# Token matmuls of an attention block in one run with two heads side by side, and the first loads reordered

## The chip, the cores and the metric

The kernel runs on one core of one Trainium2 chip. The metric is the device time of one execution, in microseconds (us); the median of ten runs is given. A profiled execution of the same kernel gives the trace that is read below: for each engine its instructions, their start, their duration and what they waited for. TensorE does matmuls, VectorE (DVE), ScalarE (ACT) and GpSimd (POOL) do the element work, SyncE (SP), ACT and GpSimd issue DMAs on their own queues, and instructions of one engine run in the order in which they are written.

## The reference

Linear attention without a softmax, a norm per head, and then a bilinear feed-forward layer:

```python
kv = einsum('bhsd,bhse->bhde', k, v)        # B 8, H 8, S 576, D 64
o = einsum('bhsd,bhde->bhse', q, kv)
o = o / sqrt(mean(o * o, axis=-1) + 1e-6) * g_norm
x = o.transpose(0, 2, 1, 3).reshape(4608, 512)
out = ((x @ w_a) * (x @ w_b)) @ w_out       # 512 -> 1536 -> 512
```

All inputs and the output are fp32; the kernel computes in bf16 with fp32 sums.

## The kernel before, in words

The output is made in nine strips of 512 tokens; a batch has 576 tokens, so strip s+1 needs the first tokens of batch s+1 and the last ones of batch s. The matrix that all strips read is `xt`: x transposed, 128 rows by 4 blocks by 4608 tokens, in bf16. The FFN of a strip is 12 units (`Unit`, n = 0 to 11) of two halves of four 128x512 matmuls each (L315): half a ends in a copy by ACT (L329, `part_a`), half b in a multiply by DVE (L333, `part_b`). Then come four output groups (n = 12 to 15, `ffn_o`, 12 matmuls each, L372), whose copies alternate between DVE and ACT and whose rows SP stores (L365). The PSUM memory has eight banks, `P[:, 0]` to `P[:, 7]`. From strip 1 on, the halves of the units take banks 1, 2, 0, 4 in turn (`ab_bank`), output groups bank 3 (`O`) or the next of the turn.

Batches 0 and 1 are made up front with q transposed by TensorE. Of pair 0 (two heads) of batch 0, q, k and v come as fp32 on SP's and ACT's queues and are cast by DVE and ACT (L447 to L450); the other pairs come in bf16 on GpSimd's queue (`load_pair`, three DMAs at L116 for each), which also makes the identity matrix that the transposes need (`make_identity`, a memset and a select). While TensorE waits at the start it runs matmuls of zeros (`dummy`, L400).

Batches 2 to 7 are made inside strips 1 to 6, batch s+1 in strip s, by `slot(A, s, n)`: it is called after each unit or output group n, and as `slot(A, s, n - 0.5)` between its two halves, and what it issues stands at that place in every engine's order. At n = k0 TensorE makes kv of one batch, in strips 3 and 5 of two (`kv`, L168, pairs of 128x64 tiles, into bank 7); copies put it on the diagonal of `kvb`, a 128x128 matrix per pair of heads with zeros elsewhere (`kv_out`, L179). The attention output is made in five chunks of tokens (0 to 3 of 128, and LC = 4 of the last 64): `tx` multiplies a chunk of q with `kvb`, four 128x128 matmuls (L265), and ACT squares the result (L272); `tss` sums the squares per head on DVE (L276); `trs` takes the reciprocal root on ACT (L281) and multiplies with g on GpSimd (L288); `txt` multiplies on DVE (L297) into `x_tok` and SP transposes it into `xt` by DMA (L299). The chunks' `tx` come at n = 6.5, 8, 9.5, 11, 12.5 in strip 1; in the strips 2 to 6 at x0, x0+1.5, +2.5, +4, +5 with x0 = 3.5, 5.5, 1.5, 5.5, 1.5. `tss` follows half a step, `trs` one and `txt` two and a half steps after `tx`. The banks of the chunks are 5, 6, 7 in turn.

At n = 12, 4, 8, 5, 8 of strips 1 to 5, after that step's slot, SP also issues the transposition of the next batch's q from DRAM (`transpose_q`, L151), and at n = 3 and 14 of strip 1 and at n = 10, 14, 8 of strips 2 to 4 GpSimd issues the loads of a later batch (`load_late`: a copy that waits for a transposition, L136, and six DMAs, L139 to L146).

Of the kernel before, what the change touches and what calls it, by code (L numbers as in the profile page):

```python
# [8 lines left out]
FP32 = mybir.dt.float32  # L9
BF16 = mybir.dt.bfloat16  # L10
AF = mybir.ActivationFunctionType
# [4 lines left out]
def kernel(  # L16
# [11 lines left out]
    nc = tc.nc  # L28

    B, H, S, D = q.shape  # L30
# [5 lines left out]
    NP = H // 2  # L36
    HF = S // 2
    STRIP = 512
# [10 lines left out]
    def sb(shape, dt, name):  # L49
        return pool.tile(shape, dt, name=name, tag=name)  # L50
# [11 lines left out]
    LC = S // 128  # L62
# [14 lines left out]
    k_x = sb([128, 2 * EC * D], FP32, "k_x")  # L77
    k32 = k_x[0:EP].rearrange("p (h c d) -> p h c d", h=2, c=EC)

    sqt = [sb([128, H, D], FP32, f"sqt{i}") for i in range(2)]  # L80
    sqt.append(k_x[:, 0 : H * D].rearrange("p (h d) -> p h d", h=H))
    sst = [sb([128, H], FP32, f"sst{i}") for i in range(3)]
    rst = [sb([128, H], FP32, f"rst{i}") for i in range(3)]
    g_all = sb([128, D], FP32, "g_all")
# [2 lines left out]
    ident = sb([128, 128], BF16, "ident")  # L87
# [7 lines left out]
    q32, v32 = (t[0:EP].rearrange("p (h c d) -> p h c d", h=2, c=EC) for t in qv)  # L95
# [9 lines left out]
    P = psum.tile([128, 8, STRIP], FP32, name="P", tag="P")  # L105
    O = 3
# [8 lines left out]
    def load_heads(b, t, src, hs):  # L115
        nc.gpsimd.dma_start(  # L116
            out=t[:, hs, :, :], in_=src[b, hs].rearrange("h (t c) d -> t h c d", c=EC)
        )

    def load_pair(b, p):  # L120
        hs = slice(2 * p, 2 * p + 2)
        load_heads(b, qt[b], q, hs)
        load_heads(b, kt[b], k, hs)
        load_heads(b, vt[b], v, hs)
# [8 lines left out]
    def load_late(b):  # L133
        if b > EARLY:

            nc.gpsimd.tensor_copy(gate, qT[(b - 1) % 2][0:1, 0, 0:1])  # L136
        d = qs_d[b].rearrange("t (h d) -> t h d", h=H)
        for hs in (slice(0, NP), slice(NP, H)):
            nc.gpsimd.dma_start(out=d[:, hs, :], in_=q[b, hs].rearrange("h t d -> t h d"))  # L139
        n = 128 * LC  # L140
        for t, src in ((ktl[b % 2], k), (vtl[b % 2], v)):
            nc.gpsimd.dma_start(
                out=t[:, :, 0:LC, :],
                in_=src[b, :, 0:n].rearrange("h (t c) d -> t h c d", c=LC),
            )
            nc.gpsimd.dma_start(  # L146
                out=t[0 : S - n, :, LC, :], in_=src[b, :, n:].rearrange("h t d -> t h d")
            )

    def transpose_q(b):  # L150
        nc.sync.dma_start_transpose(qT[b % 2], qs_d[b])  # L151


    class Attn:
# [101 lines left out]
            t0 = min(c * 128, S - 128)  # L256
            return t0, slice(c * 128 - t0, 128)

        def by_head(self, i):
            return P[:, i, :].rearrange("t (h d) -> t h d", h=H)  # L260

        def tx(self, c, i):
            t0, r = self.rows(c)
            for p in range(NP):
                nc.tensor.matmul(  # L265
                    P[:, i, p * 128 : (p + 1) * 128],
                    lhsT=self.qT[:, p, t0 : t0 + 128],
                    rhs=kvb[self.b % 2][:, p, :],
                    start=True,
                    stop=True,  # L270
                )
            nc.scalar.activation(sqt[c % 3][r], self.by_head(i)[r], AF.Square)  # L272

        def tss(self, c):
            _, r = self.rows(c)
            nc.vector.reduce_sum(sst[c % 3][r], sqt[c % 3][r], axis=mybir.AxisListType.X)  # L276

        def trs(self, c):
            _, r = self.rows(c)
            n = r.stop - r.start  # L280
            nc.scalar.activation(  # L281
                rst[c % 3][r],
                sst[c % 3][r],
                AF.Abs_reciprocal_sqrt,
                bias=eps_t[r],
                scale=1.0 / D,
            )
            nc.gpsimd.tensor_mul(  # L288
                sqt[c % 3][r],
                rst[c % 3][r].unsqueeze(2).to_broadcast([n, H, D]),  # L290
                g_all[r].unsqueeze(1).to_broadcast([n, H, D]),
            )

        def txt(self, c, i):
            t0, r = self.rows(c)
            t = x_tok[c // 3][:, c % 3]
            nc.vector.tensor_mul(t[r], self.by_head(i)[r], sqt[c % 3][r])  # L297
            t0 += self.b * S
            nc.sync.dma_start_transpose(  # L299
                xt[:, :, t0 + r.start : t0 + 128], t[r].rearrange("t h d -> t (h d)")  # L300
            )


    class Unit:
        n = 0
# [30 lines left out]
            self.part_a(kcs)  # L336
            self.part_b(kcs)

    AB = (4, 1, 2, 0)
    n_ab = [0]  # L340

    def ab_bank():
        n_ab[0] += 1
        return AB[(n_ab[0] - 1) % len(AB)]

    def ffn_ab(s, fc, between=None):
        u = Unit(s, fc, ab_bank(), ab_bank())
        u.part_a()
        if between:
            between()  # L350
        u.part_b()
# [38 lines left out]
    def ffn_o(s, g, i=O, between=None):  # L390
        o_mm(s, g, i, range(FC // 2))
        if between:
            between()
        o_mm(s, g, i, range(FC // 2, FC))
        o_out(s, g, i)
# [8 lines left out]
    def pair_src(src, p):  # L404
        return src[0, 2 * p : 2 * p + 2].rearrange("h (t c) d -> t h c d", c=EC)

    g_src = g_norm.rearrange("(u d) -> u d", u=1)
    make_identity(nc, ident)
    nc.sync.dma_start(out=q32, in_=pair_src(q, 0))
    nc.scalar.dma_start(out=k32, in_=pair_src(k, 0))  # L410
    nc.vector.memset(zeros, 0.0)
    nc.sync.dma_start(out=v32, in_=pair_src(v, 0))
    nc.scalar.dma_start(out=g_row[:, 0:D], in_=g_src)
    nc.scalar.dma_start(out=g_row[:, D : 2 * D], in_=g_src)
    nc.vector.memset(eps_t, EPS)
    nc.vector.memset(one, 1.0)
    nc.scalar.activation(warm, eps_t, AF.Abs_reciprocal_sqrt)
    nc.vector.memset(ones, 0.0)
    for t in kvb:
# [2 lines left out]
        nc.vector.memset(t[S - 128 * LC :, :, LC, :], 0.0)  # L422
    nc.vector.memset(ones[0:D, 0:D], 1.0 / D)
    nc.vector.memset(ones[D : 2 * D, D : 2 * D], 1.0 / D)
    for p in range(1, NP):
        load_pair(0, p)
    WC = 256
    for c in range(0, KC, 2):
# [13 lines left out]
    A = Attn(0)  # L442
# [9 lines left out]
    t = P[:, 2, :].bitcast(BF16)[:, 0:S].rearrange("q (c t) -> q c t", c=EC)  # L452
# [4 lines left out]
    for c in range(EC):  # L457
        nc.tensor.matmul(
            P[:, SS, 0 : 2 * D],
            lhsT=kc0[:, c, :],  # L460
            rhs=vc[:, c, :],
            start=(c == 0),
            stop=(c == EC - 1),
        )
    for j in range(2):
        r = slice(j * D, (j + 1) * D)
# [7 lines left out]
    for p in range(1, NP):  # L474
        i = X[p % 2]
# [34 lines left out]
    u3.part_a()  # L510
    u2.part_b()
    u3.part_b()
    n_ab[0] = 0
    for fc in range(4, FC):
        ffn_ab(0, fc)

# [1 line left out]
    A = Attn(1)  # L518
# [25 lines left out]
    u1.first((0, 1, 2))  # L544
    u0.rest((3,))
    u1.rest((3,))
    n_ab[0] = 1


    def slot(A, s, n):  # L550

        kb = P[:, 7, :].rearrange("q (b p e) -> q b p e", b=2, e=D)
        if s == 1:
            k0, xs = 5, (6.5, 8, 9.5, 11, 12.5)
        else:
            k0, x0 = {2: (2, 3.5), 3: (4, 5.5), 4: (0, 1.5), 5: (4, 5.5), 6: (0, 1.5)}[s]
            xs = tuple(x0 + x for x in (0, 1.5, 2.5, 4, 5))

        if n == k0 and s in (1, 2, 3, 5):
            two = [A] if s < 3 else [A, Attn(s + 2)]  # L560
            for i, a in enumerate(two):
                for p in range(NP):
                    a.kv(p, kb[:, i, p, :])
            for i, a in enumerate(two):
                a.kv_out(slice(0, NP), kb[:, i], nc.vector.tensor_copy if i else nc.scalar.copy)
        for c, x in enumerate(xs):
            i = 5 + c % 3
            if n == x:
                A.tx(c, i)
            elif n == x + 0.5:  # L570
                A.tss(c)
            elif n == x + 1:
                A.trs(c)
            elif n == x + 2.5:
                A.txt(c, i)

    for s in range(1, N_STRIP - 1):
        b = s + 1
        A = Attn(b) if b < B else None
        for n in range(FC + 4):  # L580
            amid = (lambda n=n: slot(A, s, n - 0.5)) if A else None
            if n >= FC:
                ffn_o(s, n - FC, ab_bank() if n % 2 else O, amid)
            elif s > 1 or n > 1:
                ffn_ab(s, n, amid)
            if A:
                slot(A, s, n)

            if s == 1 and n == 3:
                load_late(3)  # L590
            if b + 1 < B and n == (12, 4, 8, 5, 8)[s - 1]:
                transpose_q(b + 1)
            if b + 2 < B and n == (14, 10, 14, 8)[s - 1]:
                load_late(b + 2)
    last = N_STRIP - 1
    for fc in range(FC):
# [41 lines left out]
```

## Time and profile before

| what | us |
|---|---|
| median of ten runs | 315.94 (315.72 to 316.80) |
| the profiled execution | 315.9 |
| its span, first to last instruction | 314.1 |
| TensorE matmuls busy | 308.5 (98%) |
| DVE busy | 141.4 (45%) |
| ACT busy | 115.8 (37%) |
| GpSimd busy | 101.8 (32%) |
| 120 token matmuls of 128x128, L265, each as long as | 0.219 |
| granted TensorE clock | 1.000 of full |

A busy span counts a matmul from its start to its end; the matmuls of a stream overlap, so the distance between two starts is less than one's length, and the length of a chain of them is read from the chain's pieces. An instruction that waits is found by the idle time ahead of it and what ended that. DMAs have two times: how long the queue's engine was busy with issuing one, and how long from the issue to its landing.

### The profile page before, as it was taken

To read this page: it belongs to the slowest core of one execution; us is meant where nothing else is said; L and a number is where in the kernel's file an instruction comes from. 1 tells how busy PE (TensorE), PEld (TensorE's weight loads), DVE (VectorE), ACT (ScalarE), POOL (GpSimd) and SP (SyncE) were. 2 spreads that over 40 slices of the span, in tenths; PEclk is the share of its full clock that TensorE was granted. 3 is DMA by queue.
4 is the path that set the end of the run, shared out by engine and by line. 5 is a ranking of instruction groups with operands and counts; after the bars stand their busy time and mean duration, and the time that the engine had idled before them with its cause. 6 is when DMAs were issued, how large, how long until landed. Compare 5 with 4: busy or idle time off the path is not lost.

```text
span 314.1 us, 4977 instructions
## 1 busy us (share of the span) xinstructions
PE 308.5 (98%) x1907; PEld 147.8 (47%) x1907; DVE 141.4 (45%) x234; ACT 115.8 (37%) x225; POOL 101.8 (32%) x124
## 2 busy tenths in 40 slices
PE   7999999999999999999999999999999999999995
PEld 3444454454445444554454445544544444444443
DVE  4544335456337703583377123761683134214321
ACT  3643255353246313461364024622651233123310
POOL 8954991192453730148138300320230000000000
PEclk9999999999999999999999999999999999999999
DMA  8999999999999899059998980073022200030002
GB/s 176 198 196 199 201 186 159 229 132 162 178 168 191 80 201 150 2 61 167 204 124 124 177 168 2 19 159 109 3 50 60 102 0 0 33 102 1 0 34 102
DMA packets 94237, 36.19 MB, mean 115 GB/s; under 512 B 64902, under 2 KB 89734, under 8 KB 94214
## 3 DMA queue, kind: packets, MB, share of 16 engines
q0 software_dynamic: 59120, 18.44, 54.1%
q1 hardware_dynamic: 34738, 17.01, 24.5%
q10 hardware_dynamic: 356, 0.43, 0.5%
q8 instruction: 15, 0.25, 0.3%
q14 instruction: 8, 0.07, 0.1%
HBM read 37.78 MB, written 12.98 MB: 162 GB/s over the span
## 4 chain that ended last, share of the span: by engine, by line
PE 95%; DMA 4%; issue 0%; POOL 0%; ACT 0%; POOLq 0%
PE P L315 60%; PE P L372 30%; PE P L265 2%; DMA vt<-in_v_dram 2%; DMA qt<-in_q_dram 2%; PE P L168 2%; PE P L219 1%; PE P L192 0%; PE P L245 0%; PE P L206 0%; ACT o_end L606 0%; POOL ident masks.py:199 0%; POOL ident masks.py:197 0%; POOLq masks.py:199 0%; POOLq L622 0%
## 5 line engine op out<-in xcount | busy, mean ns | idle before, releaser
L333 DVE TENSOR_TENSOR ab<-P,asb 128x512 bf16<-128x512 f32 x108 | 74.5, 691 | 103.3 <-PE P L315 87.2
L315 PE MATMUL P<-xt,wa_t 128*128 128x512 bf16 x432 | 111.9, 379 | 0.0
L315 PE MATMUL P<-xt,wb_t 128*128 128x512 bf16 x432 | 111.7, 379 | 0.0
L329 ACT CAST asb<-P 128x512 bf16<-128x512 f32 x108 | 63.0, 585 | 92.4 <-PE P L315 92.4
L372 PE MATMUL P<-wo_t,ab 128*128 128x512 bf16 (+1 forms) x444 | 95.8, 373 | 0.0
L372 PEld LDWEIGHTS <-ab 128*128 128x128 bf16 x444 | 43.0, 98 | 48.6
L315 PEld LDWEIGHTS <-wa_t 128*128 128x128 bf16 x432 | 41.4, 98 | 47.4 <-issue 0.2
L315 PEld LDWEIGHTS <-wb_t 128*128 128x128 bf16 x432 | 41.6, 98 | 46.9 <-DMA wb_t<-in_moe_w_b_dram 0.2
L288 POOL TENSOR_TENSOR sqt<-rst,g_all 128x512 f32<-128x512 f32 (+1 forms) x24 | 25.0, 1043 | 95.9 <-ACT rst L281 95.9
L385 ACT COPY osb<-P 128x512 f32<-128x512 f32 x17 | 9.9, 585 | 67.6 <-PE P L372 63.0
L387 DVE COPY osb<-P 128x512 f32<-128x512 f32 x18 | 12.5, 692 | 44.1 <-PE P L372 39.5
L139 POOL DMA_DIRECT2D qs<-in_q_dram x12 | 19.8, 1653 | 1.1 <-issue 0.9
L276 DVE TENSOR_REDUCE sst<-sqt 128x8 f32<-128x512 f32 (+1 forms) x24 | 16.3, 680 | 2.0 <-ACT sqt L272 1.4
L297 DVE TENSOR_TENSOR qv<-P,sqt 128x512 bf16<-128x512 f32 (+1 forms) x24 | 16.4, 685 | 0.3
L272 ACT ACTIVATE sqt<-P 128x512 f32<-128x512 f32 (+1 forms) x24 | 14.4, 599 | 4.2 <-PE P L265 4.1
L265 PEld LDWEIGHTS <-qT 128*128 128x128 bf16 x120 | 9.2, 98 | 7.1
L265 PE MATMUL P<-kvb,qT 128*128 128x128 bf16 x120 | 11.6, 219 | 0.0
L281 ACT ACTIVATE rst<-sst,eps_t 128x8 f32<-128x8 f32 (+1 forms) x30 | 9.0, 301 | 4.5 <-DVE sst L276 4.3
L233 DVE SCALAR_TENSOR_TENSOR xt<-P,g_col,rs 128x288 bf16<-128x288 f32 x16 | 7.5, 511 | 5.4 <-ACT rs L223 5.4
L288 POOL TENSOR_TENSOR k_x<-rst,g_all 128x512 f32<-128x512 f32 x6 | 6.3, 1042 | 8.9 <-ACT rst L281 8.9
L131 POOL DMA_DIRECT2D wo_t<-in_moe_w_out_dram x12 | 6.4, 531 | 6.7 <-DMA wb_t<-in_moe_w_b_dram 3.3
L179 ACT CAST kvb<-P 64x64 bf16<-64x64 f32 (+1 forms) x16 | 4.6, 284 | 10.3 <-PE P L168 10.3
(67 smaller groups left out, 121.3 us busy)
## 6 DMA issues: line engine op xcount, KB each, us to landing
out_dram<-osb SPq DMA_DIRECT2D x23, 256.0 KB, 2.2
qs<-in_q_dram POOLq DMA_DIRECT2D x12, 288.0 KB, 7.0
ktl<-in_k_dram POOLq DMA_DIRECT2D x6, 512.0 KB, 9.1
vtl<-in_v_dram POOLq DMA_DIRECT2D x6, 512.0 KB, 11.4
out_dram<-osb SPq DMA_DIRECT2D x13, 128.0 KB, 2.5
wo_t<-in_moe_w_out_dram POOLq DMA_DIRECT2D x12, 128.0 KB, 6.0
wa_t<-in_moe_w_a_dram POOLq DMA_DIRECT2D x5, 256.0 KB, 8.7
wb_t<-in_moe_w_b_dram POOLq DMA_DIRECT2D x5, 256.0 KB, 9.3
```

Source lines behind the costliest of these rows:

```text
L139: nc.gpsimd.dma_start(out=d[:, hs, :], in_=q[b, hs].rearrange("h t d -> t h d"))
L265: nc.tensor.matmul(P[:, i, p * 128 : (p + 1) * 128], lhsT=self.qT[:, p, t0 : t0 + 128], rhs=kvb[self.b % 2][:, p, :], start=True, stop=True,)
L272: nc.scalar.activation(sqt[c % 3][r], self.by_head(i)[r], AF.Square)
L276: nc.vector.reduce_sum(sst[c % 3][r], sqt[c % 3][r], axis=mybir.AxisListType.X)
L288: nc.gpsimd.tensor_mul(sqt[c % 3][r], rst[c % 3][r].unsqueeze(2).to_broadcast([n, H, D]), g_all[r].unsqueeze(1).to_broadcast([n, H, D]),)
L297: nc.vector.tensor_mul(t[r], self.by_head(i)[r], sqt[c % 3][r])
L315: nc.tensor.matmul(self.a if w is wa_t else self.b, lhsT=w[:, kc, self.fc * 128 : (self.fc + 1) * 128], rhs=xt[:, kc, t0 : t0 + STRIP], st ...
L329: nc.scalar.copy(self.t, self.a)
L333: nc.vector.tensor_mul(abt[self.s % 2][self.fc], self.b, self.t)
L372: nc.tensor.matmul(P[:, i, e0:e1], lhsT=abt[s % 2][fc][:, g * 128 : (g + 1) * 128], rhs=wo_t[:, fc, e0:e1], start=(fc == 0), stop=(fc == F ...
L385: nc.scalar.copy(t, P[:, i, :])
L387: nc.vector.tensor_copy(t, P[:, i, :])
```

## The change

It has two parts. At the start, GpSimd issues the three loads of pair 1 first, then makes the identity (whose memset is now DVE's), then loads pairs 2 and 3; v of pair 0 comes in two halves, one on SP's and one on ACT's queue.

In strips 1 to 6, the five chunks are multiplied in one run at n = x0, the last chunk first: it goes to bank 3 as before, with four 128x128 matmuls by `kvb`. Chunks 0 to 3 are made by heads: each head's q (64 rows of `qT`) is multiplied with its own 64x64 kv (`kvs`, which DVE now also copies out of bank 7), so a pair of heads is two matmuls with 64 rows of contraction and 64 columns, head 0 of each pair into bank 4 or 5, head 1 into bank 6 or 7 (`place`). The squares (`tsq`) follow at x0 + 0, 1.5, 3, 4.5, 6 for chunks LC, 0, 1, 2, 3; the sums at x0 + 1, 2, 4, 5, 7; `trs` half a step and `txt` one and a half steps after the sum. x0 is 6.5, 3.5, 6.5, 1.5, 6.5, 1.5 in strips 1 to 6; k0 of strips 3 and 5 goes from 4 to 5. The units' halves take three banks in turn (0, 1, 2) instead of four; all copies of kv to `kvb` are ACT's; `load_late` goes from n = 10 to 11 in strip 2 and from 8 to 9 in strip 4. `transpose_q` keeps its places.

```diff
--- before.py
+++ after.py
@@ -77,8 +77,8 @@
     k_x = sb([128, 2 * EC * D], FP32, "k_x")
     k32 = k_x[0:EP].rearrange("p (h c d) -> p h c d", h=2, c=EC)
 
-    sqt = [sb([128, H, D], FP32, f"sqt{i}") for i in range(2)]
-    sqt.append(k_x[:, 0 : H * D].rearrange("p (h d) -> p h d", h=H))
+    sqt = [sb([128, 2, NP, D], FP32, f"sqt{i}") for i in range(2)]
+    sqt.append(k_x[:, 0 : H * D].rearrange("p (j h d) -> p j h d", j=2, h=NP))
     sst = [sb([128, H], FP32, f"sst{i}") for i in range(3)]
     rst = [sb([128, H], FP32, f"rst{i}") for i in range(3)]
     g_all = sb([128, D], FP32, "g_all")
@@ -256,45 +256,76 @@
             t0 = min(c * 128, S - 128)
             return t0, slice(c * 128 - t0, 128)
 
-        def by_head(self, i):
-            return P[:, i, :].rearrange("t (h d) -> t h d", h=H)
-
-        def tx(self, c, i):
-            t0, r = self.rows(c)
+
+        def place(self, c):
+            return tuple((4 + 2 * j + c // 2, c % 2 * (STRIP // 2)) for j in range(2))
+
+
+        def by_head(self, c):
+            if c == LC:
+                return P[:, O, :].rearrange("t (p j d) -> t j p d", j=2, p=NP)
+            (i, c0), (j, _) = self.place(c)
+            o = P[:, i : j + 1 : j - i, c0 : c0 + STRIP // 2]
+            return o.rearrange("t j (p d) -> t j p d", p=NP)
+
+
+
+        def tx(self):
             for p in range(NP):
                 nc.tensor.matmul(
-                    P[:, i, p * 128 : (p + 1) * 128],
-                    lhsT=self.qT[:, p, t0 : t0 + 128],
+                    P[:, O, p * 128 : (p + 1) * 128],
+                    lhsT=self.qT[:, p, S - 128 : S],
                     rhs=kvb[self.b % 2][:, p, :],
                     start=True,
                     stop=True,
                 )
-            nc.scalar.activation(sqt[c % 3][r], self.by_head(i)[r], AF.Square)
+            for c in range(LC):
+                t0, _ = self.rows(c)
+                for p in range(NP):
+                    for j, (i, c0) in enumerate(self.place(c)):
+                        r = slice(j * D, (j + 1) * D)
+                        nc.tensor.matmul(
+                            P[:, i, c0 + p * D : c0 + (p + 1) * D],
+                            lhsT=self.qT[r, p, t0 : t0 + 128],
+                            rhs=self.kvs[r, p, :],
+                            start=True,
+                            stop=True,
+                        )
+
+        def tsq(self, c):
+            _, r = self.rows(c)
+            nc.scalar.activation(sqt[(c + 1) % (LC + 1) % 3][r], self.by_head(c)[r], AF.Square)
 
         def tss(self, c):
             _, r = self.rows(c)
-            nc.vector.reduce_sum(sst[c % 3][r], sqt[c % 3][r], axis=mybir.AxisListType.X)
+            nc.vector.reduce_sum(
+                sst[(c + 1) % (LC + 1) % 3][r],
+                sqt[(c + 1) % (LC + 1) % 3][r].rearrange("t j p d -> t (j p) d"),
+                axis=mybir.AxisListType.X,
+            )
 
         def trs(self, c):
             _, r = self.rows(c)
             n = r.stop - r.start
             nc.scalar.activation(
-                rst[c % 3][r],
-                sst[c % 3][r],
+                rst[(c + 1) % (LC + 1) % 3][r],
+                sst[(c + 1) % (LC + 1) % 3][r],
                 AF.Abs_reciprocal_sqrt,
                 bias=eps_t[r],
                 scale=1.0 / D,
             )
             nc.gpsimd.tensor_mul(
-                sqt[c % 3][r],
-                rst[c % 3][r].unsqueeze(2).to_broadcast([n, H, D]),
+                sqt[(c + 1) % (LC + 1) % 3][r].rearrange("t j p d -> t (j p) d"),
+                rst[(c + 1) % (LC + 1) % 3][r].unsqueeze(2).to_broadcast([n, H, D]),
                 g_all[r].unsqueeze(1).to_broadcast([n, H, D]),
             )
 
-        def txt(self, c, i):
+        def txt(self, c):
             t0, r = self.rows(c)
             t = x_tok[c // 3][:, c % 3]
-            nc.vector.tensor_mul(t[r], self.by_head(i)[r], sqt[c % 3][r])
+            nc.vector.tensor_mul(
+                t[r].rearrange("t (p j) d -> t j p d", j=2), self.by_head(c)[r], sqt[(c + 1) % (LC + 1) % 3][r]
+            )
             t0 += self.b * S
             nc.sync.dma_start_transpose(
                 xt[:, :, t0 + r.start : t0 + 128], t[r].rearrange("t h d -> t (h d)")
@@ -336,12 +367,11 @@
             self.part_a(kcs)
             self.part_b(kcs)
 
-    AB = (4, 1, 2, 0)
-    n_ab = [0]
+    ab_banks = [4, 1, 2, 0]
 
     def ab_bank():
-        n_ab[0] += 1
-        return AB[(n_ab[0] - 1) % len(AB)]
+        ab_banks.append(ab_banks.pop(0))
+        return ab_banks[-1]
 
     def ffn_ab(s, fc, between=None):
         u = Unit(s, fc, ab_bank(), ab_bank())
@@ -405,15 +435,19 @@
         return src[0, 2 * p : 2 * p + 2].rearrange("h (t c) d -> t h c d", c=EC)
 
     g_src = g_norm.rearrange("(u d) -> u d", u=1)
-    make_identity(nc, ident)
     nc.sync.dma_start(out=q32, in_=pair_src(q, 0))
     nc.scalar.dma_start(out=k32, in_=pair_src(k, 0))
+    load_pair(0, 1)
     nc.vector.memset(zeros, 0.0)
-    nc.sync.dma_start(out=v32, in_=pair_src(v, 0))
+
+    nc.sync.dma_start(out=v32[:, 0:1], in_=pair_src(v, 0)[:, 0:1])
+    nc.scalar.dma_start(out=v32[:, 1:2], in_=pair_src(v, 0)[:, 1:2])
     nc.scalar.dma_start(out=g_row[:, 0:D], in_=g_src)
     nc.scalar.dma_start(out=g_row[:, D : 2 * D], in_=g_src)
     nc.vector.memset(eps_t, EPS)
     nc.vector.memset(one, 1.0)
+    nc.vector.memset(ident, 0.0)
+    make_identity(nc, ident, nomemset=True)
     nc.scalar.activation(warm, eps_t, AF.Abs_reciprocal_sqrt)
     nc.vector.memset(ones, 0.0)
     for t in kvb:
@@ -422,7 +456,7 @@
         nc.vector.memset(t[S - 128 * LC :, :, LC, :], 0.0)
     nc.vector.memset(ones[0:D, 0:D], 1.0 / D)
     nc.vector.memset(ones[D : 2 * D, D : 2 * D], 1.0 / D)
-    for p in range(1, NP):
+    for p in range(2, NP):
         load_pair(0, p)
     WC = 256
     for c in range(0, KC, 2):
@@ -510,7 +544,6 @@
     u3.part_a()
     u2.part_b()
     u3.part_b()
-    n_ab[0] = 0
     for fc in range(4, FC):
         ffn_ab(0, fc)
 
@@ -544,7 +577,7 @@
     u1.first((0, 1, 2))
     u0.rest((3,))
     u1.rest((3,))
-    n_ab[0] = 1
+    ab_banks[:] = [0, 1, 2]
 
 
     def slot(A, s, n):
@@ -556,23 +589,28 @@
             k0, x0 = {2: (2, 3.5), 3: (4, 5.5), 4: (0, 1.5), 5: (4, 5.5), 6: (0, 1.5)}[s]
             xs = tuple(x0 + x for x in (0, 1.5, 2.5, 4, 5))
 
+        k0, x0 = {1: (5, 6.5), 2: (2, 3.5), 3: (5, 6.5), 4: (0, 1.5), 5: (5, 6.5), 6: (0, 1.5)}[s]
         if n == k0 and s in (1, 2, 3, 5):
             two = [A] if s < 3 else [A, Attn(s + 2)]
             for i, a in enumerate(two):
                 for p in range(NP):
                     a.kv(p, kb[:, i, p, :])
             for i, a in enumerate(two):
-                a.kv_out(slice(0, NP), kb[:, i], nc.vector.tensor_copy if i else nc.scalar.copy)
-        for c, x in enumerate(xs):
-            i = 5 + c % 3
-            if n == x:
-                A.tx(c, i)
-            elif n == x + 0.5:
+                nc.vector.tensor_copy(a.kvs, kb[:, i])
+                a.kv_out(slice(0, NP), kb[:, i])
+        if n == x0:
+            A.tx()
+
+        for i, c in enumerate((LC, *range(LC))):
+            m = n - x0
+            if m == 1.5 * i:
+                A.tsq(c)
+            if m == (1, 2, 4, 5, 7)[i]:
                 A.tss(c)
-            elif n == x + 1:
+            if m == (1, 2, 4, 5, 7)[i] + 0.5:
                 A.trs(c)
-            elif n == x + 2.5:
-                A.txt(c, i)
+            if m == (1, 2, 4, 5, 7)[i] + 1.5:
+                A.txt(c)
 
     for s in range(1, N_STRIP - 1):
         b = s + 1
@@ -590,7 +628,7 @@
                 load_late(3)
             if b + 1 < B and n == (12, 4, 8, 5, 8)[s - 1]:
                 transpose_q(b + 1)
-            if b + 2 < B and n == (14, 10, 14, 8)[s - 1]:
+            if b + 2 < B and n == (14, 11, 14, 9)[s - 1]:
                 load_late(b + 2)
     last = N_STRIP - 1
     for fc in range(FC):
```

## The prediction

> **What bounds it now.** The page's chain of the work that ended last comes first: it names the engine.
>
> ```profile
> PE 95%; DMA 4%; issue 0%; POOL 0%; ACT 0%; POOLq 0%
> ```
>
> So TensorE sets the end, apart from a start that DMAs set. The same chain in order of time (start, length in us, what) prices the pieces:
>
> ```profile
> 1.50 5.72 DMA qt<-in_q_dram
> 7.22 0.28 issue
> 7.51 5.75 DMA vt<-in_v_dram
> 13.26 0.04 issue
> 13.30 0.38 PE P L168 x12
> ...
> 61.07 0.75 PE P L168 x40
> 61.82 2.70 PE P L315 x12
> 64.52 0.22 PE P L265 x4
> 64.74 2.59 PE P L315 x12
> ...
> 77.07 0.22 PE P L265 x4
> 77.29 6.47 PE P L372 x30
> 83.77 5.18 PE P L315 x24
> ...
> 125.45 1.39 PE P L168 x80
> ```
>
> From 13.30 on TensorE never waits: what adds or saves time there does so one for one. Four token matmuls (L265) cost 0.22. Forty kv matmuls cost 0.75 and eighty 1.39, so forty more cost 0.64, 16 ns each, and 0.11 is fixed on entry; the FFN piece that follows is 2.70 where its twin is 2.59, 0.11 more on exit. Strip 2 begins at 83.77 with no wait.
>
> The third view is SyncE's timeline ahead of that point, because strip 2 reads x that DMA transposes write:
>
> ```profile
> 76.53 1.11 SPq L365 DMA_DIRECT2D out_dram<-osb  x2
> 77.74 1.26 SPq L299 DMA_TRANSPOSE xt<-qv  x1
> 79.17 2.25 SPq L151 DMA_TRANSPOSE qT<-qs  x1
> 81.51 0.99 SPq L365 DMA_DIRECT2D out_dram<-osb  x2
> 82.59 1.24 SPq L299 DMA_TRANSPOSE xt<-qv  x1
> ```
>
> The transposition at 77.74 is chunk 2 of batch 2, tokens 1408 to 1535, the last 128 columns of strip 2. The one at 82.59 is chunk 3, first read in strip 3; it stands behind the transposition of q and two stores. Asked for line 299 around 82.6 alone, the trace gives its time from issue to landing:
>
> ```profile
> DMA to landing us min/median/max: 4.0/4.0/4.0
> ```
>
> It landed at 86.6, and nobody needed it then.
>
> **What the skill says.** The Trainium skill, TensorEngine Tiling (Array Packing), Key Properties: a change of tiling mode drains TensorE. The trace agrees: 0.11 in and 0.11 out around kv. TensorE: Matmul & The Clock Gate, Part 3: Packing small matmuls: matmuls on different row groups run together, starting about 4 ns apart. The nearest thing here is the startup's four 64x64 matmuls of 288 columns (L206), which take 0.43 in all, where each lasts about 0.29: four starts within 0.14, so two and two run together. DMA: Bandwidth & Descriptors, Queues, rings and completion order: on each DMA engine descriptors of one ring are consumed in ring order; 4.0 at 82.59 behind the q transposition against a least of 2.4 over all 30 agrees.
>
> **The change, part by part.**
>
> *Start.* GpSimd's first load moves from 1.50 to about 0.74, past the identity's memset (0.20, now DVE's) and select (0.29, now behind three issues of 0.84, 0.65, 0.64: done near 3.2, wanted at 5.64). The select stands ahead of the second group of loads, which still gains 0.76-0.29. Queue traffic by window shows the software queue's first packets in 4.5 to 5.0, three us after issue, and from 5.5 on that queue alone at about 195 GB/s written. So the gain is the gap filled, not the whole 0.76: 4.0 to 5.5 ran at 264, 241 and 226 GB/s after 326, with a tail on SP's queue alone (v). V in halves lets both fp32 queues carry that tail; the earlier software packets take some of it back. The 13.30 matmul waits for vt of pair 3, so an earlier landing helps until TensorE's own chain binds: the waits there are 0.33 (8.85), 0.16 (11.11) and about 0.3 twice for qt. I take -0.45; ends +0.1 (the loads crowd v out, and with it the casts at 6.42) and -0.75. ACT's extra issue (0.44) lies before its table load, done at 3.33 plus 0.44, and k is wanted at 5.38: free; with that cover gone, 0.44. DVE's ident memset is 0.1 to 0.2 in a queue idle from 3.3 to 5.0.
>
> *Token matmuls.* Before: five groups of 0.222 per strip, 1.11. After: the last chunk the old way, 0.22; then 32 matmuls, two 64-row tiles in pairs on different banks, 64 columns each. No row shows 64x128 tiles. Nearest is kv (64 columns, two column tiles): 16 ns each, 0.51, with 0.22 for entry and exit. Sum 0.95, gain 0.16 per strip, six strips: -0.96. Lower end: no drain and pairs at column speed (64 of 512 columns of a 0.216 matmul, 27 ns a pair): 0.22+0.43, -0.46 each, -2.8. Upper end: the weight loads don't overlap; six loads of 96x128 at the start take 0.28, first to last start 0.18, so 36 ns each: 32 make 1.15, total 1.59, +0.48 each, +2.9. I take -0.96, since kv's loads and matmuls overlap in just this way.
>
> *Banks.* Pairs of a and b now rotate over three banks, not four. A half unit is 4 matmuls, 0.864. ACT's copy ends 0.78 after its matmuls are issued, DVE's multiply 0.96 (0.27+0.69); the bank is wanted after two halves, 1.73: 0.77 to spare. The densest place has a chunk's multiply and the next one's sum (0.68 each) between two DVE multiplies: 0.96+1.37 = 2.33 against 2.0 when the next could start, 0.33 late, still covered. Cost nothing; uncovered, some tenths per strip. Banks 4 to 7 are free at the run's start: the kv copies (four by 0.37 on ACT after a double kv, 1.5) have 12 matmuls (2.59) of cover. The new copy to kvs (128x256, 0.42 by the like-sized row L603) lies in DVE's idle half; the second batch's two copies (0.42 on DVE) go to ACT at 0.37. Same elements in Square, sum and multiply: same durations.
>
> *Moved work.* The kv of strips 3 and 5 and their runs go one unit later, and the late loads of strips 2 and 4 too (GpSimd: gate copy, six DMAs) so that they follow the last GpSimd multiply (1.04). These loads take 9 to 11 to land, and the batch that they bring is used over 20 later: hidden. Stores and transposes keep order on SP in these strips; their needed chunks land 2 us or more ahead (strip 3's chunk 1 issued near 144.4, strip 4 starts at 150.51).
>
> *Strip 1, the path.* There x0 stays 6.5, but with the last chunk first, chunk 2's multiply falls at n=13 instead of 12. SP's order at n=12 and 13 becomes: store, chunk 1 (in the place of 77.74), the q transposition, store, chunk 2 (in the place of 82.59). The q transposition didn't move: a needed transposition has moved behind it. From the end of the n=12 matmuls (75.77) to a landing of the 82.59 kind is 86.6-75.77 = 10.8; TensorE reaches strip 2 after three output groups of 2.59, 7.8. It stands still for 3.05 whatever the earlier gains are, as both count from n=12. Queued behind: all of strip 2; DVE and ACT wait for it. Ends: landing after 2.4, stall 1.45; after 7.1, the slowest of the 30, stall 6.1.
>
> *Sum.* 314.1 - 0.45 - 0.96 + 3.05 = 315.74 of span. The profiled execution took 315.9, 1.8 around the span: 317.5. The median, 315.94, is 0.04 from that execution.
>
> **Rivals.** (1) *Short landing*, 0.13: the transposition lands after 2.4 and the stall is 1.45: 315.9, no difference. For it: most transpositions took 2.6. Against: the one in this place took 4.0. (2) *Faster*, 0.07: strip 2 scarcely waits. It needs a stall under 0.78, so chunk 2 landed within 1.7 of its issue; at none the time is 314.5. Against: 2.4 is the least of 30, and SP is in order. That the wait isn't there at all would mean that the chunk isn't needed by strip 2's first matmul; each reads all 512 columns. (3) *Weight loads bind*, 0.12: the packed run costs more than the plain one, up to +0.48 a strip: 318.5 to 321.4. Against: kv's rate. (4) *Clock*, 0.07: the skill's page on the clock gate (Part 1) has TensorE fall to half clock after an idle window of about 3.4; with 3.05 it just holds, but a landing 0.4 later could lose it, and a window at half speed costs 1.7 more: 319.5. No run here shows such a stop. The forecast keeps 0.61.
>
> **Numbers.** 0.2% (0.63 us) is about what a measurement here can tell. Slower: forecast, (3), (4): 0.80; same: (1), 0.13; faster: (2), 0.07. The range from 315.9 to 319.8 holds all but (2) and the worse half of (3). The likeliest case's own range is 316.9 to 318.4 (start and landing each by some tenths).
>
> **What would show it.** A first FFN matmul of strip 2 (L315 of before) waiting for DMA xt about 3 us, near 83 to 86, the SP timeline with chunk 2 after the q transposition, everything behind shifted. The token run as one piece near 0.95, of it 0.73 for 32 small matmuls and their drains. The first kv of pair 3 near 12.85. No waits of FFN matmuls for ACT or DVE. I am wrong if strip 2 starts without a wait, if the token run exceeds 1.1, or if the wait for pair 3 lands later than 13.3.

## The result: slower, by more than forecast

The changed kernel takes 320.86 us (median of nine executions; 318.9 to 324.91) where the kernel before takes 315.96. The ratio is 1.0137, with a 95% interval of 1.012 to 1.0154; it leaves out two executions above 323 as slow ones, and the two medians as they stand give 1.0155. The forecast was slower too, but by a third of it: 317.5, 1.6 more, where 4.9 more was measured; its range ended at 319.8. The profiled execution took 321.5 with a span of 319.7, 5.6 more than the span before. Executions whose TensorE clock stayed full took 318.9 to 319.2. In the others its mean was 0.984 to 0.995 of full; in the profiled one, with 0.995, it stood at half for 3.4 us, as shown below.

TensorE waits at two places now, where it never did after the start. Who waited for whom, on TensorE (us in total, times, longest):

```profile
PE P L346 <- DMA xt<-qv: 2.6, 1, 2.6
PE P L168 <- DMA vtl<-in_v_dram: 2.4, 2, 1.4
```

The first is the wait of strip 2 that was forecast; the second, of strip 3's kv, was not. (L346 is the FFN matmul that was L315, L402 the output matmul, L330 the transposition of a chunk that was L299, L317 the GpSimd multiply that was L288.) The chain in order of time shows the token run and both waits:

```profile
64.46 0.22 PE P L275 x4
64.68 0.57 PE P L287 x32
65.25 7.88 PE P L346 x36
73.13 7.78 PE P L402 x36
...
82.58 3.51 DMA xt<-qv
86.09 0.04 issue
86.13 5.34 PE P L346 x24
...
116.35 16.55 DMA vtl<-in_v_dram
132.90 0.04 issue
132.94 1.07 PE P L168 x18
134.01 3.75 PE P L346 x12
```

A token run is 0.22 and 0.57, and 0.11 lies in the 36 FFN matmuls behind it, which take 7.88 instead of 7.77 (three times 2.59): 0.90 against 1.11 before. Strip 2's first matmul starts at 86.13 when chunk 2 has landed. In strip 3 the load of v, issued at 116.35, is 16.55 under way, and the pieces behind it are slow: 12 FFN matmuls take 3.75, not 2.70. TensorE's timeline has the two waits of that place, 1.44 and 0.95:

```profile
129.42 0.82 PE L168 MATMUL P<-vtl,ktl 128*64 128x64 bf16 x40
131.68 0.32 PE L168 MATMUL P<-vtl,ktl 128*64 128x64 bf16 x8 [1.44 <-DMA vtl<-in_v_dram]
132.94 1.07 PE L168 MATMUL P<-vtl,ktl 128*64 128x64 bf16 x32 [0.95 <-DMA vtl<-in_v_dram]
```

The first forty are kv of batch 4 and run at once. Only the other forty, of batch 5, read the v that these loads bring: eight need only the first of the two loads, and the next one needs the second.

SyncE's timeline ahead of strip 2 has the order that was forecast:

```profile
76.48 1.11 SPq L395 DMA_DIRECT2D out_dram<-osb  x2
77.68 1.25 SPq L330 DMA_TRANSPOSE xt<-qv  x1
79.10 2.29 SPq L151 DMA_TRANSPOSE qT<-qs  x1
81.48 1.00 SPq L395 DMA_DIRECT2D out_dram<-osb  x2
82.58 1.95 SPq L330 DMA_TRANSPOSE xt<-qv  x1
```

Line for line it is the order of before, at almost the same times; but the last line is now chunk 2, which strip 2 needs.

Busy time by windows (us, length, then PE busy, PEld, DVE, ACT and POOL busy, granted clock, DMA share, GB/s) shows what follows the second wait:

```profile
131.00:132.00 1.00, 0.32 (x8) 0.20 (x8) 0.00 (x0) 0.00 (x0) 0.00 (x0) 1.00 1.33 128
132.00:133.00 1.00, 0.06 (x3) 0.06 (x4) 0.00 (x0) 0.00 (x0) 0.00 (x0) 0.85 0.72 60
133.00:134.00 1.00, 1.00 (x33) 0.94 (x33) 0.00 (x0) 0.00 (x0) 0.00 (x0) 0.50 0.00 0
134.00:135.00 1.00, 1.00 (x4) 0.37 (x4) 0.42 (x1) 0.49 (x2) 0.00 (x0) 0.50 0.00 0
135.00:136.00 1.00, 1.00 (x3) 0.30 (x2) 0.42 (x1) 0.51 (x2) 0.00 (x0) 0.50 0.00 0
136.00:137.00 1.00, 1.00 (x6) 0.48 (x5) 0.00 (x0) 0.96 (x3) 0.00 (x0) 0.94 0.00 0
```

The clock falls to half near 132.7 and is full again soon after 136. With that the 5.6 can be split by place. Strip 2 starts 2.53 later (86.13 against 83.60 in the two timelines): 0.06 gained at the start and 0.21 by strip 1's run, so 2.80 lost by the wait (the 2.6 above counts from the end of the last matmul ahead of it, these figures from start to start). Strip 4 starts 6.28 later (chain, 156.79 against 150.51): 2.53, less 0.21 for each of two runs, leaves 4.17 for strip 3. Its last 32 kv matmuls start at 132.94; without a wait it would have been 0.78 after 129.42, as before (126.16 after 125.38), so 130.20. So from start to start the two waits cost 2.74 and the half clock the other 1.43, on these 32 (1.00 to the next FFN matmul, not 0.61) and on the 12 FFN matmuls. Strips 4, 5 and 6 give 0.21 each back: -0.06 - 6 x 0.21 + 2.80 + 2.74 + 1.43 = 5.65.

Why v of batch 5 was late is in the queues that issue. GpSimd before, between its last multiply of strip 2's run and the loads of v:

```profile
105.01 1.04 POOL L288 TENSOR_TENSOR sqt<-rst,g_all 64x512 f32<-64x512 f32 x1 [1.09 <-ACT rst L281]
106.11 0.18 POOL L136 COPY gate<-qT 1x1 bf16<-1x1 bf16 x1
...
111.97 0.72 POOL L146 DMA_DIRECT2D vtl<-in_v_dram  x1
```

and in the changed kernel:

```profile
109.51 1.04 POOL L317 TENSOR_TENSOR sqt<-rst,g_all 128x512 f32<-128x512 f32 x1 [2.67 <-ACT rst L310]
110.50 0.18 POOL L136 COPY gate<-qT 1x1 bf16<-1x1 bf16 x1
...
116.35 0.73 POOL L146 DMA_DIRECT2D vtl<-in_v_dram  x1
```

The last multiply of the run, which the loads follow in GpSimd's queue, ends 4.5 later: strip 2's start gives 2.5 of it, the run's longer schedule the rest. And SyncE, in whose queue the transposition of batch 5's q stood behind a chunk of strip 3 before (it started at 137.10), finds it now ahead of that strip's first chunk, so it starts as soon as SP has issued the last stores of strip 2, at 120.11; the q that it reads had landed at 119.8:

```profile
120.29 6.39 SPq L151 DMA_TRANSPOSE qT<-qs  x1
```

That is in the middle of batch 5's loads. The two loads of v took 12.1 and 11.6 to land before, and 16.2 and 16.5 now. Before, the second landed at 123.6 and its first reader in kv, a matmul of batch 5's half, started at 126.16 in the trace: 2.55 to spare. Now the issue is 4.4 later, but kv came 4.0 later as well (129.42 for 125.38), so this takes only 0.34 of the time to spare. The landing, 4.9 longer, takes the rest and more.

### The profile page after: what moved, and what is told of

It is laid out like the page before. It is cut to its first block, busy times and chain, and to the rows that moved or that the text cites. A ratio compares the mean times of both kernels' runs of the same rounds, so it can differ in the third digit from the quotient of the medians.

```text
span 319.7 us, 5155 instructions
## 1 busy us (share of the span) xinstructions
PE 309.6 (97%) x2003; PEld 146.4 (46%) x2003; DVE 142.1 (44%) x237; ACT 117.6 (37%) x229; POOL 101.2 (32%) x123
## 4 chain that ended last, share of the span: by engine, by line
PE 84%; DMA 8%; POOL 4%; issue 1%; DVE 0%; SPq 0%; ACT 0%; POOLq 0%; DVEq 0%
PE P L346 55%; PE P L402 25%; DMA vtl<-in_v_dram 5%; DMA wb_t<-in_moe_w_b_dram 2%; PE P L168 2%; DMA xt<-qv 1%; PE P L287 1%; POOL qt L116 1%; POOL qs L139 1%; POOL vt L116 1%; PE P L192 0%; POOL wa_t L464 0%; POOL kt L116 0%; PE P L275 0%; PE P L219 0%
## 5 line engine op out<-in xcount | busy, mean ns | idle before, releaser
L346 PE MATMUL P<-xt,wa_t 128*128 128x512 bf16 x432 | 112.7, 381 | 2.6 <-DMA xt<-qv 2.6
L346 PE MATMUL P<-xt,wb_t 128*128 128x512 bf16 x432 | 112.0, 380 | 0.1
L402 PE MATMUL P<-wo_t,ab 128*128 128x512 bf16 (+1 forms) x444 | 95.6, 373 | 0.0
L346 PEld LDWEIGHTS <-wa_t 128*128 128x128 bf16 x432 | 42.0, 98 | 53.0 <-issue 3.7
L402 PEld LDWEIGHTS <-ab 128*128 128x128 bf16 x444 | 43.1, 98 | 49.1
L346 PEld LDWEIGHTS <-wb_t 128*128 128x128 bf16 x432 | 41.9, 98 | 50.7 <-issue 0.8
L317 POOL TENSOR_TENSOR sqt<-rst,g_all 128x512 f32<-128x512 f32 (+1 forms) x24 | 25.0, 1040 | 94.4 <-ACT rst L310 94.1
L417 DVE COPY osb<-P 128x512 f32<-128x512 f32 x18 | 12.4, 691 | 41.0 <-PE P L402 40.9
L179 ACT CAST kvb<-P 64x256 bf16<-64x256 f32 (+1 forms) x20 | 6.0, 301 | 16.3 <-DVE kvs L599 11.3
L317 POOL TENSOR_TENSOR k_x<-rst,g_all 128x512 f32<-128x512 f32 x6 | 6.3, 1043 | 16.8 <-ACT rst L310 16.8
L430 PE MATMUL P<-zeros 128*128 128x512 bf16 x17 | 6.8, 541 | 1.2 <-DVE eps_t L447 1.2
L168 PE MATMUL P<-vtl,ktl 128*64 128x64 bf16 x240 | 5.3, 203 | 2.4 <-DMA vtl<-in_v_dram 2.4
```

The source lines that it names most:

```text
L168: nc.tensor.matmul(o[j * D : (j + 1) * D, :], lhsT=kk[0:n, 2 * p + j, c, :], rhs=vv[0:n, 2 * p + j, c, :], start=(c == 0), stop=(c == len( ...
L317: nc.gpsimd.tensor_mul(sqt[(c + 1) % (LC + 1) % 3][r].rearrange("t j p d -> t (j p) d"), rst[(c + 1) % (LC + 1) % 3][r].unsqueeze(2).to_br ...
L346: nc.tensor.matmul(self.a if w is wa_t else self.b, lhsT=w[:, kc, self.fc * 128 : (self.fc + 1) * 128], rhs=xt[:, kc, t0 : t0 + STRIP], st ...
L402: nc.tensor.matmul(P[:, i, e0:e1], lhsT=abt[s % 2][fc][:, g * 128 : (g + 1) * 128], rhs=wo_t[:, fc, e0:e1], start=(fc == 0), stop=(fc == F ...
L417: nc.vector.tensor_copy(t, P[:, i, :])
```

## Experiments

### Strip 1's transposition of q behind chunk 2

```diff
-            if b + 1 < B and n == (12, 4, 8, 5, 8)[s - 1]:
+            if b + 1 < B and n == (13, 4, 8, 5, 8)[s - 1]:
```

> The changed kernel with strip 1's transposition of q one step later, behind chunk 2 (n = 13 for 12). Theory: the wait of 2.6 us ahead of strip 2's first matmul is only SP's order, so it goes, and the waits for vtl in strip 3 stay, with or without half clock behind them: 2.8 us less, 316.0 to 318.1 by the median. Rival A (the wait in strip 3 is a knock-on of the one in strip 2, because late loads and kv stand apart by it): both go, 314.6. Rival B (chunk 2 is late by its own making or by load on the DMA engines): the wait at strip 2 stays above 1.5 us.

Measured: 317.14, ratio to the kernel before 1.0055 (1.0033 to 1.0077). The wait of strip 2 shrank from 2.6 to 0.4, the one of strip 3 stayed:

```profile
PE P L168 <- DMA vtl<-in_v_dram: 1.2, 1, 1.2
PE P L346 <- DMA xt<-qv: 0.4, 1, 0.4
```

Strip 2's wait is thus SP's order, but for 0.4: chunk 2, now ahead of the transposition of q, still takes 3.8 to land. The wait of strip 3 is no mere knock-on of it (rival A): it goes on without it, if at half the length. The loads of v land after 13.9 and 15.1 here, though the transposition of q again starts 4.8 after the first of them is issued.

### Strip 3's transposition of q behind the run's first chunk

```diff
-            if b + 1 < B and n == (12, 4, 8, 5, 8)[s - 1]:
+            if b + 1 < B and n == (12, 4, 9, 5, 8)[s - 1]:
```

> The changed kernel with strip 3's transposition of q at n = 9 instead of 8, so that on SP's queue it stands behind the transposition of the run's first chunk, as it stood behind a chunk in the kernel before. Theory Q: in the changed kernel this transposition ran ahead, from 120 us, among the loads of batch 5, and made their landing 16 us instead of 12; held back, vtl lands about 4 us earlier, the two waits of strip 3's kv (2.4 us) and the half clock behind them go: 316.9 to 317.4. Rival L (the loads are late because they are issued a step later): the waits stay at 2 us or more and the time at 319 to 321. The wait at strip 2 stays in both.

Measured: 317.68 (1.0064, 1.0042 to 1.0086). In the profile, with a full clock throughout, the loads are issued at the same times as in the changed kernel (v at 115.50 and 116.38) but land after 12.4 and 11.9, and strip 3's kv runs as one piece of 80, as in the kernel before, in TensorE's timeline:

```profile
129.45 1.46 PE L168 MATMUL P<-vtl,ktl 128*64 128x64 bf16 x80
```

The place of one transposition is worth 4 us of landing and the whole second wait; the wait at strip 2, 2.8 here, is untouched. The loads are as late here as in the changed kernel, against the same kv at 129.45, and nothing waits for them: lateness alone is not enough.

### The late loads at n = 10

```diff
-            if b + 2 < B and n == (14, 11, 14, 9)[s - 1]:
+            if b + 2 < B and n == (14, 10, 14, 9)[s - 1]:
```

> The changed kernel with strip 2's late loads at n = 10 as in the kernel before, not 11. Rival L: they land 1.7 us or more earlier and the waits in strip 3 fall to under 0.7 us, the clock stays full: 317 to 318. Theory Q: the transposition of q comes earlier too, as it waits only for its data, and still lies among these loads; the waits stay over 1 us, time above 318.

Measured: 317.66 (1.0067, 1.0043 to 1.0092). GpSimd issues v at 113.49 and 114.36, 2.0 earlier than in the changed kernel, since the loads now stand ahead of the last multiply, and v lands after 12.7 and 13.4. Strip 3 doesn't wait, as rival L had it. That doesn't make lateness half of the cause: kv is at 131.14 here, so the loads stand 3.7 further ahead of it than in the changed kernel and 3.4 further than in the kernel before, ten times the 0.34 that the change had taken. It is a second cure. The expectation was wrong on the transposition of q: it didn't come earlier with its data, which had landed at 117.2, but at 122.01, behind the last stores of strip 2. The time isn't better than that of the experiment before, and the profiled execution shows another thing: the clock fell after the wait at strip 2, at 0.50 from 88 to 90 (the columns are those of the windows above).

```profile
83.00:86.00 3.00, 0.44 (x3) 0.10 (x1) 0.00 (x0) 0.58 (x1) 0.66 (x2) 1.00 0.69 146
86.00:88.00 2.00, 1.84 (x8) 0.85 (x8) 0.00 (x0) 0.58 (x1) 2.00 (x2) 0.87 0.81 208
88.00:90.00 2.00, 2.00 (x7) 0.63 (x5) 0.69 (x1) 0.00 (x0) 2.00 (x3) 0.50 1.56 117
90.00:92.00 2.00, 2.00 (x9) 0.86 (x8) 0.43 (x1) 0.58 (x1) 1.97 (x3) 0.78 2.06 151
```

In the changed kernel's own profile it didn't fall there: one and the same stop of about 2.7 us may or may not cost the clock, and the part on the clock below shows what decides. By the shares of these windows it is at half for 3.4 us in all (0.5 + 2.0 + 0.9), a loss of 1.7.

### Both places of the transposition

Strip 1 at n = 13 and strip 3 at n = 9, together.

> The changed kernel with both places of the transposition of q of the two experiments before (strip 1 at n = 13, strip 3 at n = 9). If both waits are SP's order, nothing waits in TensorE's steady part: 319.7 - 2.8 - 4.2 = 312.7 of span, 314.5, faster than the kernel before by 0.4%. If one of them has another cause, 316 or more.

Measured: 315.52, ratio 0.9986 (0.9978 to 0.9995), span 313.4: the sign is turned, if by 0.14% only, but 1.0 of the expected gain is missing. 0.7 of it is a wait that remains, because chunk 2 at n = 13 is late even ahead of the transposition of q:

```profile
PE P L346 <- DMA xt<-qv: 0.7, 1, 0.7
```

It is issued at 79.97 and lands 4.0 later. The median of all executions is another 0.3 above the profiled one.

### The start alone

The kernel before with the changed loads and identity at the start, and nothing else.

```diff
-    make_identity(nc, ident)
...
+    load_pair(0, 1)
...
-    nc.sync.dma_start(out=v32, in_=pair_src(v, 0))
+    nc.sync.dma_start(out=v32[:, 0:1], in_=pair_src(v, 0)[:, 0:1])
+    nc.scalar.dma_start(out=v32[:, 1:2], in_=pair_src(v, 0)[:, 1:2])
...
+    nc.vector.memset(ident, 0.0)
+    make_identity(nc, ident, nomemset=True)
...
-    for p in range(1, NP):
+    for p in range(2, NP):
```

> The kernel before with the changed start alone (loads of pair 1 ahead of the identity, v in halves). The forecast's term was -0.45. Theory after the changed kernel's trace: kv of pair 3 starts 0.35 earlier, but a weight chunk that lands at the pace of the software queue takes it back, so 0 to -0.15: 315.8 to 316.0. If the forecast's term is right and the changed kernel lost it elsewhere, 315.5.

Measured: 315.95 against 315.92, ratio 0.9999 (0.9991 to 1.0008). The start is worth nothing that can be measured. The changed kernel's trace shows why in two lines, GpSimd's first load and the chain:

```profile
1.29 0.83 POOL L116 DMA_DIRECT2D qt<-in_q_dram  x1 [0.85 <-POOLq L660]
```

```profile
9.95 6.50 DMA wb_t<-in_moe_w_b_dram
16.45 0.05 issue
16.50 18.95 PE P L346 x87
```

The load began 0.21 earlier, not 0.76: with the identity gone from ahead of it, most of the time that it took is issue time for which the profile shows no cause (0.66 in the chain). Nor did the queue move data earlier for it: the first packet of GpSimd's queue is at 4.80 in the kernel before and at 4.88 in the changed one. Pair 3's kv still started 0.35 earlier (12.95 for 13.30), but a weight chunk landed at 16.45 and the FFN matmul that it feeds ran at 16.50, 0.11 before its time of before (16.61).

### The run issued twice

The mended kernel (both orders), with the 32 small matmuls of each run issued a second time into the same places.

```diff
-            for c in range(LC):
+            for c in (*range(LC), *range(LC)):
```

> The kernel with both orders of q's transposition mended (e4), where the 32 small matmuls of each run are issued twice into the same places; nothing else changes. It prices one of them without the change of tiling: at the 16 ns of the forecast 6 x 0.51 = 3.1 us more than e4's 315.5, at column speed (27 ns a pair) 6 x 0.43 = 2.6; if the drains are nearly free and the matmuls cost all of the 0.57 of a run, 3.4.

Measured: 317.4 (1.0051, 1.0035 to 1.0066), 1.9 above the mended kernel. The time alone would mislead: in its profile chunk 2 landed 2.6 after its issue and strip 2 didn't wait, so the mended kernel's 0.7 is missing on the other side. The price is read from TensorE's timelines; first the changed kernel, then this one:

```profile
64.61 0.64 PE L287 MATMUL P<-kvs,qT 64*128 64x64 bf16 x32
```

```profile
64.76 1.11 PE L287 MATMUL P<-kvs,qT 64*128 64x64 bf16 x64
```

Thirty-two more take 0.47, 14.7 ns each, 29 for a pair, and six runs 2.8. With the 0.7 taken off, 2.1 of the spans' 2.3 (315.7 against 313.4) is explained. At column speed (64 of the 512 columns of a 0.216 matmul) one of them alone would need 27, and two in turn 54, so the two of a pair run side by side, weight loads included.

### Chunk 2 ahead of an unmoved transposition

The changed kernel with strip 1's kv and run a unit earlier, and strip 3's transposition at n = 9. Chunk 2 is then at n = 12.

```diff
-        k0, x0 = {1: (5, 6.5), 2: (2, 3.5), 3: (5, 6.5), 4: (0, 1.5), 5: (5, 6.5), 6: (0, 1.5)}[s]
+        k0, x0 = {1: (4, 5.5), 2: (2, 3.5), 3: (5, 6.5), 4: (0, 1.5), 5: (5, 6.5), 6: (0, 1.5)}[s]
...
-            if b + 1 < B and n == (12, 4, 8, 5, 8)[s - 1]:
+            if b + 1 < B and n == (12, 4, 9, 5, 8)[s - 1]:
```

> The changed kernel with strip 1's kv and run one unit earlier (k0 4, x0 5.5), so that chunk 2 is at n = 12, ahead of the transposition of q, which keeps its place there; strip 3's transposition at n = 9 as before in this study. The last wait of strip 2, 0.7 with the transposition behind chunk 2 at n = 13, goes too: span 312.7, time 314.5, faster than the kernel before by 0.45%. If the first chunk's GpSimd multiply, which now falls nearer to the late loads' issue, holds DVE and with it a bank, some tenths come back: 315.

Measured: 314.68 against 315.92, ratio 0.9963 (0.995 to 0.9975). This version beats both kernels: 1.2 less than before, 6 less than the changed one. TensorE's timeline enters strip 2 without a wait:

```profile
80.63 3.19 PE L402 MATMUL P<-wo_t,ab 128*128 128x512 bf16 x14
83.65 1.03 PE L346 MATMUL P<-xt,wa_t 128*128 128x512 bf16 x4
```

After the start, a wait of 0.2 for a load of v is all that TensorE has left for a DMA. The span, 313.1, is 1.0 below that of before; the token runs alone would give 1.26.

### Order alone, and lateness alone, on the kernel before

The kernel before with strip 3's transposition of q ahead of the run's first chunk:

```diff
-            if b + 1 < B and n == (12, 4, 8, 5, 8)[s - 1]:
+            if b + 1 < B and n == (12, 4, 7, 5, 8)[s - 1]:
```

> The kernel before with strip 3's transposition of q at n = 7 instead of 8, so that on SP it stands ahead of the run's first chunk. Order alone, no lateness: it starts near 118, when its data are there, among batch 5's loads. If order alone costs 3 to 4.5 us of landing, vtl lands at 126.6 to 128 instead of 123.6 and kv at 125.4 waits 0.8 to 2.3: 316.8 to 318.3, more where the clock falls. If order matters only together with the lateness, no wait and 315.9.

Measured: 316.01 against 316.05, ratio 0.9995 (0.9987 to 1.0004). The transposition starts at 118.04, v lands after 13.0 and 13.3 instead of 12.1 and 11.6, and kv doesn't wait. The 3 to 4.5 that I expected for the order was wrong here: it costs 0.9 to 1.7, and the time to spare hides it. The second load lands at 125.68, after the piece of 80 kv matmuls has started at 125.45, and still nothing waits: the first forty of it don't read this v. Nor was it order without lateness. GpSimd's gate copy waited 0.28 for the transposition of the batch before, so from the issue of the last load to the start of kv there are 13.07 us, just as in the changed kernel (13.41 in the kernel before).

And the kernel before with the late loads a step later in the program:

```diff
-            if b + 2 < B and n == (14, 10, 14, 8)[s - 1]:
+            if b + 2 < B and n == (14, 11, 14, 8)[s - 1]:
```

> The kernel before with strip 2's late loads at n = 11 instead of 10. Lateness alone: GpSimd issues them one unit, 1.73 us, later; they had 1.85 us to spare (123.6 against 125.4), so a wait of 0 to 0.3 and 315.9 to 316.3. A wait of more than 1 us would say that lateness alone is enough.

Measured: 315.99, ratio 0.9995 (0.9985 to 1.0004). The expectation rested on a false step: the loads did not move by 1.73. The gate copy ran at 106.27 for 106.11, because nothing stood between n = 10 and n = 11 in GpSimd's queue. The number n sets only an order; the lateness in the changed kernel comes from the multiply that now lies ahead. So lateness alone was not tried by this kernel; it was by the changed kernel with strip 3's transposition held back, which didn't wait there.

## Why the prediction was wrong

**The bound** (TensorE's one-for-one) held, and so did the sign.

**Strip 1, the path**: right. The place, the order on SP and the price were as forecast, 2.80 for 3.05; the landing was 3.5 after the issue where 4.0 was taken. The first experiment shows the cause by undoing it. What the runs don't bear out is the reason given for a landing of 4.0, that the transposition of q stands ahead: with chunk 2 ahead of it the landing took 3.8, 4.0 and 2.6 in three kernels.

**Token matmuls**: right in mechanism, a little small in size. A small matmul costs 14.7 ns, not 16, and entry and exit together 0.21 where 0.22 was taken (0.57 less 0.47 for 32 of them, and 0.11 behind the run): 0.79 + 0.11 for a run against 0.95, so 0.21 a strip and 1.26 in all, where the sum had 0.96. The weight loads did not bind, which was rival (3).

**Banks**: right. No FFN matmul waits for ACT or DVE with three banks. (Bank 3 for the last chunk is new: by the code it had bank 6 before.)

**Start**: wrong. The term -0.45 is -0.06 in the trace, and nothing can be measured of it alone. The step that failed: "an earlier landing helps until TensorE's own chain binds". What binds behind it is the software queue again, one weight chunk later. I had also taken the issue to move from 1.50 to 0.74; it moved to 1.29.

**Moved work**: the step that failed, and that took the time past 319.8. It put this term at nothing on two grounds. One was that "stores and transposes keep order on SP in these strips". `transpose_q` does keep its places, n = 8 in strip 3, but the run moved by a unit, and its first chunk with it, from n = 8 to 9: the transposition of batch 5's q, which had started at 137.10 behind that chunk, started at 120.29 ahead of it, among batch 5's loads. I had asked the question of strip 1's transposition and not of strip 3's, where it isn't the queue that suffers but the loads. The other ground was that loads that take 9 to 11 to land, for a batch used over 20 later, are hidden. The last load of v took 11.6 already before, and had 2.55 to spare when it landed; its landing of 16.5 used up more than that. Waits that cost 2.74 came of it, and the half clock, 1.43, came behind them. Holding the transposition back takes both away, and so do loads issued well earlier. That the other terms would have come to 317.3 (321.5 less these two), near the 317.5 forecast, is luck in part: the start was off by +0.39, the token runs by -0.30 and strip 1 by -0.25.

**Clock**: rival (4) named the mechanism and put 1.7 on it, with a chance of 0.07; it cost 1.43 in the profiled execution, behind strip 3's waits. It was thought to need a stop longer than 3.05. Two stops of 1.44 and 0.95, with 0.3 of work between them, were enough, and one of about 2.7 was in another kernel. The Trainium skill's page TensorE: Matmul & The Clock Gate, Part 1, says that the clock falls after an idle window of about 3.4 us; the stops here were shorter and the fall is the same kind, so the window isn't to be taken as a safe length of a stop.

The traces show what decides. The granted clock changes only at steps of 3.41 us: in the changed kernel its record starts at 6.41, falls to half at 132.70 and rises at 136.12; with the late loads at n = 10 it starts at 5.55, falls at 87.47 and rises at 90.89. That is 37 steps and 1, and 24 and 1. Cut at these steps, the windows of the changed kernel are

```profile
81.50:84.92 3.42, 1.99 (x10) 0.78 (x8) 0.73 (x2) 0.58 (x1) 0.00 (x0) 1.00 1.05 228
84.92:88.33 3.41, 2.20 (x11) 1.01 (x11) 0.20 (x1) 0.58 (x1) 3.04 (x3) 1.00 0.72 160
129.29:132.70 3.41, 1.27 (x49) 0.94 (x49) 0.69 (x1) 0.00 (x0) 0.00 (x0) 1.00 1.14 86
132.70:136.12 3.42, 3.18 (x38) 1.74 (x38) 0.85 (x2) 1.10 (x4) 0.00 (x0) 0.50 0.01 1
```

and with the late loads at n = 10

```profile
84.06:87.47 3.41, 1.31 (x7) 0.60 (x7) 0.00 (x0) 0.25 (x2) 2.13 (x3) 1.00 0.69 151
87.47:90.89 3.42, 3.42 (x10) 1.22 (x9) 0.69 (x1) 0.92 (x2) 3.42 (x4) 0.50 1.58 138
```

The clock fell after steps with 1.27 and 1.31 of busy TensorE, 2.1 idle. It held at strip 2 of the changed kernel, whose stop lies across two steps, with 1.4 and 1.2 idle. The most idle step that it stood was one of 1.63, at the end of the kernel before (309.00 to 312.41). So in these traces a stop of 2.7 costs the clock or not by where it falls on the steps.

With the terms put right, and a full clock, the sum is 314.1 - 0.06 - 1.26 + 2.80 + 2.74 + 1.8 around the span = 320.1, 1.0 to 1.2 above what the executions with a full clock took; what their waits were is not in a trace.

What stays open: why an early transposition of q costs 3.8 and 4.6 of landing in the changed kernel and 0.9 to 1.7 in the kernel before. It starts 4.8 after the first load of v is issued in the one and 6.5 in the other, so more of the loads lie behind it; but in the first experiment it starts 4.8 after as well, and the loads land after 13.9 and 15.1, not 16.2 and 16.5. Where it starts is at most part of the answer.

## What to carry to other kernels

A DMA issue that moves past another is moved for everyone behind it: list the queue's new order by place, and for each item ask both who needs it and whose transfer it now shares the engines with. Count the time to spare of a load from its landing in the trace to the first instruction that reads it (a merged piece of 80 can have its first reader in the middle), never from the step that issues it, and take off it every delay that the change makes, together, less what its reader is delayed. A program step number isn't a time: an engine's instruction moves only if something that takes time comes to stand ahead of it.

## What the runs showed of the hardware

- Two matmuls of 64 rows and 64 columns with 128-column weights, into two PSUM banks, run side by side at 29 ns a pair, weight loads included.
- GpSimd's queue moved its first packet between 4.77 and 4.95 in all eleven traces, whether its first load was issued at 1.50 or at 1.29.
- TensorE's clock fell to half after waits of 1.44 and 0.95 in a row, and in another kernel after one of about 2.7; both times it was back after 3.41, at a cost of 1.4 and 1.7. It did not fall after the changed kernel's own stop at strip 2, of the same length. In these traces it changes only at steps of 3.41; it fell after a step with 2.1 idle and held after steps with up to 1.63.
- A DMA transposition that starts among loads from DRAM delays them: 16.2 and 16.5 of landing for 12.4 and 11.9, with the loads' own issue times unchanged. A second pair of kernels, with chunk 2 ahead in strip 1, gives 13.9 and 15.1 for 12.0 and 11.6, and a third, on the kernel before, 13.0 and 13.3 for 12.1 and 11.6.
